# One load queue, single PSUM banks and head groups: a change to a selective-attention and MLP-mixer kernel

## The chip, the cores and the metric

The kernel runs on one core of a Trainium2 chip. The core has five engines that run side by side and wait for one another through semaphores: TensorE (PE in the profile; PEld are its weight loads), VectorE (DVE), ScalarE (ACT), GpSimd (POOL) and SyncE (SP). Transfers between memory and SBUF run on 16 DMA engines; here they are issued from two places, SP (the hardware queue, q1 in the profile) and GpSimd (the software queue, q0). Products of TensorE go to PSUM, eight banks of 512 f32 a partition, and are taken out of it by VectorE or ScalarE. The metric is device microseconds of one execution, lower is better. All times are in microseconds (us) unless another unit stands with them.

## What is computed

Eight batches, eight heads, sequence 576, head dimension 64, model dimension 512. The output of the attention is the input of a mixer block.

```
s_pos  = maximum(s, 0);  cum = cumsum(s_pos, axis=-1)
scores = q @ k^T / 8                                  # causal
scores = scores + minimum(-(cum_i - cum_j), 0)
attn   = softmax(scores)                              # 1e-9 in the denominator
x      = (attn @ v) with heads side by side           # (8, 576, 512)

h   = relu(x^T @ w_tok1) @ w_tok2                     # token mixing, 576 -> 256 -> 576
u   = x + h^T
out = u + relu(u @ w_ch1) @ w_ch2                     # channel mixing, 512 -> 1536 -> 512
```

Inputs and output are f32.

## The kernel before

**How the order is made.** The kernel does not write its instructions in order. It gives operations to a planner (`Plan`, L53): each with the engines that could do it, a cost and a latency for each, what it reads and writes, a priority, and for loads the time on the DMA engines. `Plan.run` (L103) simulates the engines and one DMA stream and picks operation after operation. The instructions are then issued in that order (L1023 to L1031), and each engine executes its own in that fixed order; semaphores keep it right when reality differs from the plan. Buffers come from rings (`Ring`, L21) of a few tiles each: `qkn` 5, `vf` 2, `E` 4, `x` 3 in SBUF, and in PSUM `psc`, two tiles of two banks (L434), and `pmx`, four tiles of one bank (L435). Where TensorE would be idle in the first 45 us of the plan, filler products of zeros are put in (L1002 to L1022).

**Work of a batch.** A quad is four heads. For each quad, one DMA from GpSimd brings k and one q, cast to bf16 (`load_cast`, L448; 288 KB written, 256 rows). TensorE transposes them in 64x64 blocks into one `psc` tile for two pairs of heads (L645); ScalarE or VectorE evicts each half (L655, L657). Scores of a pair of heads go to `psc` in two pieces (L679); ScalarE takes the exponential into `E` (L687) and VectorE applies the causal mask (L693, L701). The factor exp(cum_j) is multiplied into v instead of the scores: v comes in five chunks of 128 (the last 64) sequence rows (`vf`, L581; 256 KB and 1024 rows of 256 bytes, the last 128 KB) and is multiplied by the factor `wT` into `vp` (L590), with the factor itself as a further column (L601, L603), so that the value product (L722) gives the denominator too. The value products of two heads go into one `psc` tile, and a reciprocal (L728) and a multiplication normalise them into `x`: for batch 0 one head on VectorE (L742) and one, in five pieces, on ScalarE (L737), for later batches both in one instruction (L748).

`tok` (L792) does the token mixing: products of `w1` with x (L810), for batches 0 and 1 in two groups of four heads, relu into `h` (L820, L821), the products with `w2` in both layouts (L833 and L843 transposed, evicted at L855 and L857; L867 with the addition L874). `chan` (L906) does the channel mixing: products with `wc1` (L921), relu (L928, L930), products with `wc2` (L939), addition (L950) and store from SP (L955, L958). The channel work of a batch is what TensorE interleaves with the attention of the next.

**Queues around the change.** GpSimd issues, in this order: k and q of batch 0, then the gate, then the token weights in four pieces (512, 64, 256 and 256 rows; the keys w1, w1e, w2, w2e), wc1 in four pieces (256 rows each) and wc2 in four (384 rows each), then k and q of batches 1 to 7, and last those of batches 0 and 1 once more, for a sum of squares (L607) that a range check needs. The gate (L759) is a copy of one element of v's third chunk on GpSimd; the token weights come behind it. v is loaded by SP in all batches. For batches 1 to 7 a one-element memset of the `vf` buffer on GpSimd (L571) stands in the GpSimd order ahead of v, and the SP load waits for it. SP also issues the stores and, from batch 2 on, the transposing DMAs (L883). The load of s (L497) is the first on SP. From it come the running sum `cum`, its exponential `wn` (L516, ScalarE), and `wT` by transposes on TensorE (L524, L527). A further scan of `wn` (`pre`, L547) and four small comparisons (`gaps`, L551) belong to the same range check, which is evaluated at the end.

## Time and profile before

| what | value |
|---|---|
| time, median of 3 runs | 316.18 us (315.94 to 317.01) |
| the profiled execution's own time | 316.02 us |
| its span, first to last instruction | 314.2 us |
| granted TensorE clock, mean | 0.995 |
| DMA | 38.69 MB in 72284 packets, of which 53936 under 512 bytes |

The profile is of one execution. Busy time is the union of an engine's instructions; a row of the timeline gives start, length, engine, line, operation, tiles, shape and count, and in brackets how long the engine had been idle and what released it. A row by stage gives, for each engine, busy time and the count of instructions, then the granted clock, the DMA engines' busy share (packets that overlap count each, so it can pass 1) and GB/s written. For a DMA the page has the issuing instruction's length and, apart from it, the time from issue to landing. The share of a queue is the time that its packets took over 16 engines and the span.

### The profile page before, as it was taken

What the parts mean: (1) busy time and instruction counts of PE and PEld (TensorE: products, weight loads), DVE (VectorE), ACT (ScalarE), POOL (GpSimd) and SP (SyncE); (2) the same over time, 40 slices, a digit from 0 to 9 for tenths busy, and PEclk for the clock granted to TensorE, in tenths of its full rate; (3) what the DMA queues carried; (4) which work ended last, traced back from release to release, by engine and by line L of the source; (5) the groups of instructions that cost most, each with busy time, mean ns of one, the idle gap of its engine ahead of it and who ended that gap; (6) DMA issues with size and microseconds to landing.
All of it is one profiled execution on the core that took longest, in us unless ns stands there. A gap on an engine that the chain in (4) does not pass through costs nothing.

```text
span 314.2 us, 8013 instructions
## 1 busy us (share of the span) xinstructions
PE 293.0 (93%) x3350; PEld 168.1 (53%) x3390; DVE 168.2 (54%) x354; ACT 187.1 (60%) x315; POOL 79.5 (25%) x121
## 2 busy tenths in 40 slices
PE   4888999989999999999999999999999999999991
PEld 1446774468574455445674455446764554447540
DVE  5583235679866655586566547676425744330020
ACT  2777687858976559644783649658763356108400
POOL 5294342495247010601035010820000000000000
PEclk9999999999999999999999999999999999999997
DMA  7999999999999839346908743693003310150032
GB/s 141 180 132 204 196 198 198 214 201 248 209 203 143 180 90 216 47 100 156 187 5 132 149 104 53 102 177 121 2 0 69 102 67 2 49 136 35 1 103 73
DMA packets 72284, 38.69 MB, mean 123 GB/s; under 512 B 53936, under 2 KB 67568, under 8 KB 72240
## 3 DMA queue, kind: packets, MB, share of 16 engines
q1 hardware_dynamic: 57520, 22.57, 32.7%
q0 software_dynamic: 14720, 15.54, 31.8%
q8 instruction: 28, 0.46, 0.6%
q14 instruction: 16, 0.13, 0.1%
HBM read 40.65 MB, written 9.44 MB: 159 GB/s over the span
## 4 chain that ended last, share of the span: by engine, by line
PE 83%; DVE 6%; ACT 4%; DMA 2%; issue 2%; POOL 0%; ACTq 0%; DVEq 0%; POOLq 0%
PE pmx L939 28%; PE pmx L921 28%; PE psc L679 6%; PE pmx L810 6%; PE pmx L867 5%; PE psc L722 4%; PE psc L645 3%; DMA qkn<-in_q_dram 2%; ACT qT L655 2%; DVE qT L657 1%; ACT E L687 1%; DVE x L748 1%; DVE kT L657 1%; PE pmx L843 1%; PE pmx L1018 1%
## 5 line engine op out<-in xcount | busy, mean ns | idle before, releaser
L687 ACT ACTIVATE E<-psc 128x1024 bf16<-128x1024 f32 x64 | 62.9, 1024 | 32.6 <-PE psc L679 27.8
L921 PEld LDWEIGHTS <-wc 128*128 128x128 bf16 x624 | 58.4, 98 | 31.2 <-issue 1.0
L921 PE MATMUL pmx<-uTb,wc 128*128 128x320 bf16 (+2 forms) x384 | 55.9, 299 | 0.0
L939 PE MATMUL pmx<-wc,gb 128*128 128x512 bf16 x231 | 54.0, 379 | 0.6 <-issue 0.2
L928 ACT ACTIVATE gb<-pmx 128x320 bf16<-128x320 f32 (+2 forms) x69 | 30.3, 441 | 26.9 <-PE pmx L921 22.2
L590 POOL TENSOR_TENSOR vp<-vf,wT 128x512 bf16<-128x512 f32 (+1 forms) x35 | 36.0, 1047 | 40.0 <-issue 20.2
L921 PE MATMUL pmx<-uTa,wc 128*128 128x512 bf16 (+1 forms) x232 | 43.9, 335 | 0.8 <-issue 0.6
L939 PE MATMUL pmx<-wc,ga 128*128 128x512 bf16 x179 | 43.3, 380 | 1.2 <-issue 0.8
L607 ACT ACTIVATE junk<-qkn 128x1152 bf16<-128x1152 bf16 x32 | 37.2, 1163 | 0.4
L939 PEld LDWEIGHTS <-gb 128*128 128x128 bf16 x240 | 22.5, 98 | 25.9 <-issue 0.2
L928 ACT ACTIVATE ga<-pmx 128x512 bf16<-128x512 f32 (+1 forms) x49 | 24.2, 500 | 19.8 <-PE pmx L921 18.9
L693 DVE TENSOR_TENSOR E<-E,keep 128x512 bf16<-128x512 bf16 x64 | 28.5, 450 | 12.1 <-ACT E L687 11.9
L450 POOL DMA_DIRECT2D qkn<-in_q_dram x20 | 14.4, 718 | 59.7 <-PE psc L645 51.8
L939 PEld LDWEIGHTS <-ga 128*128 128x128 bf16 x192 | 17.3, 98 | 20.4 <-issue 1.3
L679 PE MATMUL psc<-qT,kT 64*128 64x256 bf16 (+2 forms) x320 | 23.4, 256 | 2.9 <-ACT qT L655 1.1
L722 PEld LDWEIGHTS <-E 128*128 128x128 bf16 x576 | 21.2, 97 | 8.5 <-issue 3.1
L722 PE MATMUL psc<-vp,E 128*128 128x65 bf16 x576 | 22.4, 193 | 2.8 <-ACT x L737 1.2
L748 DVE TENSOR_TENSOR x<-psc,rc 128x640 bf16<-128x640 f32 x28 | 23.1, 824 | 0.9
L679 PEld LDWEIGHTS <-kT 64*128 64x128 bf16 x320 | 12.9, 95 | 19.1 <-issue 16.5
L950 DVE TENSOR_TENSOR of<-pmx,ua 128x512 f32<-128x512 f32 x16 | 10.9, 689 | 19.1 <-PE pmx L939 19.1
L450 POOL DMA_DIRECT2D qkn<-in_k_dram x20 | 14.9, 745 | 18.4 <-issue 9.2
L810 PE MATMUL pmx<-x,w 128*128 128x512 bf16 (+1 forms) x97 | 19.2, 336 | 0.3 <-DVE x L748 0.2
(83 smaller groups left out, 263.2 us busy)
## 6 DMA issues: line engine op xcount, KB each, us to landing
vf<-in_v_dram SPq DMA_DIRECT2D x32, 256.0 KB, 6.6
out_dram<-of SPq DMA_DIRECT2D x32, 256.0 KB, 2.2
qkn<-in_k_dram POOLq DMA_DIRECT2D x20, 288.0 KB, 6.0
qkn<-in_q_dram POOLq DMA_DIRECT2D x20, 288.0 KB, 7.5
wc<-in_moe_w_ch_dram POOLq DMA_DIRECT2D x8, 384.0 KB, 11.2
vf<-in_v_dram SPq DMA_DIRECT2D x8, 128.0 KB, 5.2
out_dram<-of SPq DMA_DIRECT2D x8, 128.0 KB, 3.2
w<-in_moe_w_tok_dram POOLq DMA_DIRECT2D x2, 256.0 KB, 4.5
```

What stands on the lines that cost most here:

```text
L450: nc.gpsimd.dma_start(out=n.t[:, i, :, :], in_=src[b, h : h + 4, :, :].rearrange("(f e) (p r) d -> (e p) f (r d)", e=2, r=R))
L590: eng.tensor_tensor(out=vp.t[p0 : p0 + n, c, :, 0:D], in0=vf.t[p0 : p0 + n, c, :, :], in1=wT[p0 : p0 + n, cw, b * H : b * H + H].unsqueeze ...
L607: nc.scalar.activation(out=junk[:, :].rearrange("p (t n) -> p t n", t=2), in_=i, func=AF.Square, accum_out=sq[:, col : col + 1])
L679: nc.tensor.matmul(out=ps.t[:, hh * 512 + c0 : hh * 512 + c0 + e - a], lhsT=kT.t[hh * 64 : hh * 64 + 64, j0 : j0 + 128], rhs=qT.t[hh * 64 ...
L687: nc.scalar.activation(out=E.t[:, :, 512 * pc : 512 * pc + 512], in_=ps.t[:, :].rearrange("p (e n) -> p e n", e=2), func=AF.Exp, scale=0.125)
L693: nc.vector.tensor_tensor(out=o, in0=o, in1=keep[:, :].unsqueeze(1).unsqueeze(1).to_broadcast([128, 2, 2, 128]), op=ALU.mult)
L722: nc.tensor.matmul(out=o[:, hh, ic, 0 : D + 1], lhsT=E.t[:, hh, d0 : d0 + 128], rhs=vp.t[:, jc, h + 2 * hh, 0 : D + 1], start=(jc == j_lo) ...
L748: nc.vector.tensor_tensor(out=x.t[:, :, :].rearrange("p c (g f e d) -> p g e f c d", f=2, e=2, d=D)[:, h // 4, h % 2], in0=pav()[:, :, :, ...
L810: nc.tensor.matmul(out=pm.t[:, ha * D : hb * D], lhsT=w1[:, NJ if odd and c == NJ - 1 else c, t * 128 : t * 128 + 128], rhs=x.t[:, c, ha * ...
L921: nc.tensor.matmul(out=pm.t[:, 0 : e - a], lhsT=wc1[:, m, cc * 128 : cc * 128 + 128], rhs=uT.t[:, m, a:e], start=(m == 0), stop=(m == NMC ...
L928: lambda cc=cc, pm=pm, a=a, e=e: nc.scalar.activation(out=g.t[:, cc, a:e], in_=pm.t[:, 0 : e - a], func=AF.Relu),
L939: nc.tensor.matmul(out=pm.t[:, :], lhsT=g.t[:, cc, c * 128 : c * 128 + 128], rhs=wc2[:, cc, :], start=(cc == 0), stop=(cc == NCC - 1))
```

## The change

1. **One queue.** All loads but two go through one order on GpSimd: k and q of batch 0, v of batch 0, token weights, wc1, k and q of batch 1's first quad, half of wc2, the second quad, the other half, v of batch 1, and then per batch k/q, v, k/q. The two that stay on SP are s and the last, half-sized v chunk of batch 0, which is now SP's second load. The gate and the memsets go. In the plan each load also depends on the landing of the load eight places ahead.
2. **Single banks.** In batch 0 the transposes of one k or q go into two `pmx` tiles, one for each pair of heads, instead of one `psc` tile; the value products of the first quad go into a `pmx` tile for each head. In all of batch 0 each head has its own reciprocal and its own normalisation, on either engine (the plan's cost for ScalarE is 1.05 instead of 0.6).
3. **Token products by head groups.** In batches 0 and 1 the groups of L810 are heads 0 to 3, heads 4 and 6, heads 5 and 7; relu is done for each half of the columns, and a transposed `w2` product waits for its half alone.
4. **Smaller ones.** v products of batch 0 may go to GpSimd; `wn` has a higher priority; the copy `w1s` (L767) a later one, and even batches no longer wait for it; the scan `pre` and `gaps` are placed after the last eviction of batch 1's token stage; the planner's start time of GpSimd is 1.25 instead of 0.5.

```
-    def load_op(fn, key, us):
-        last[0] = P.op({"SP": (0.6, 0, fn)}, writes=key, prio=1, dma=us, after=last[0])
-    def cast_op(fn, key, us, occ=0.75, prio=-1):
-        last[1] = P.op({"POOL": (occ, 0, fn)}, writes=key, prio=prio, dma=us, after=last[1])
+    def load_op(fn, key, us, occ=0.75, prio=-1):
+        o = P.op({"POOL": (occ, 0, fn)}, writes=key, prio=prio, dma=us, after=chain[-1] if chain else None)
+        if len(chain) >= 8:
+            o.deps.add(chain[-8])
+        chain.append(o)
...
-        if b:
-            last[1] = P.op({"POOL": (0.1, 0.2, lambda: nc.gpsimd.memset(vf.t[0:1, 0, 0, 0:1], 0.0))},
-                           writes=[(vf, 0)], prio=-1, after=last[1])
...
             def load(c=c, n=n, p0=p0):
-                nc.sync.dma_start(out=vf.t[p0 : p0 + n, c, :, :],
+                nc.gpsimd.dma_start(out=vf.t[p0 : p0 + n, c, :, :],
                                   in_=v[b, :, c * 128 : c * 128 + n, :].rearrange("h p d -> p h d"))
+            if b == 0 and c == NJ - 1:
+                P.op({"SP": (0.6, 4.6, load_first)}, writes=[(vf, c)], prio=-2)
+                continue
...
-            pt = Buf(r_sc, False)
+            pts = [Buf(r_mx, False) for e in range(2)] if b == 0 else [Buf(r_sc, False)] * 2
...
-        pa, rc = Buf(r_sc, False), Buf(r_rc, False)
+        apart = b == 0 and h < 4
+        pas, rc = [Buf(r_mx, False) for hh in range(2)] if apart else [Buf(r_sc, False)] * 2, Buf(r_rc, False)
...
+        if b == 0:
+            for hh in range(2):
+                def rcp(hh=hh):
+                    nc.vector.reciprocal(out=rc.t[:, hh, :], in_=pav(hh)[:, :, D])
+                P.op({"DVE": (0.2, 0.25, rcp)}, reads=[(pas[hh], hh)], writes=[(rc, hh)], prio=0)
...
+                P.op({**dve(320, nrm), "ACT": (1.05, 1.2, nrm_a)}, reads=[(pas[hh], hh), (rc, hh)],
+                     writes=[(x, h + 2 * hh)], prio=-1)
+            return
...
-        heads = [(0, 4), (4, H)] if b < 2 else [(0, H)]
+        heads = [(0, 4), (4, 6), (5, 7)] if b < 2 else [(0, H)]
...
+        rgroups = [(0, 4), (4, 8)] if b < 2 else [(0, H)]
...
-    gate((vbuf[0][0], 2), lambda: vbuf[0][0].t[0:1, 2, 0, 0:1])
     load_tok()
     for i in range(4):
         load_ch1(i)
-    for i in range(4):
+    stage_qk(1, 0)
+    for i in range(2):
         load_ch2(i)
-    for b in range(1, B):
-        for h in range(0, H, 4):
-            if b > 1 or h >= AHEAD:
-                stage_qk(b, h)
-            if h == 0:
-                stage_v(b)
+    stage_qk(1, 4)
+    for i in range(2, 4):
+        load_ch2(i)
+    stage_v(1)
+    for b in range(2, B):
+        stage_qk(b, 0)
+        stage_v(b)
+        stage_qk(b, 4)
```

## What was predicted, before the result

> **What bounds the kernel now.** I read the first part of the page, then busy time by stage, then the chain of waits, and only then single rows of the first 32 us.
>
> ```profile
> PE 293.0 (93%) x3350; PEld 168.1 (53%) x3390; DVE 168.2 (54%) x354; ACT 187.1 (60%) x315; POOL 79.5 (25%) x121
> ...
> core 0: us, PE busy (x) PEld busy (x) DVE busy (x) ACT busy (x) POOL busy (x), PEclk, DMA share, GB/s
> 0.00:31.64 31.64, 23.37 (x340) 13.83 (x345) 18.37 (x58) 19.54 (x40) 17.66 (x36) 1.00 0.98 164
> 31.64:82.70 51.06, 47.65 (x719) 32.27 (x724) 31.05 (x63) 38.95 (x67) 23.41 (x34) 1.00 1.18 209
> 82.70:281.80 199.10, 196.08 (x2143) 106.93 (x2169) 114.64 (x228) 118.10 (x186) 38.43 (x52) 1.00 0.54 106
> ...
> 0.00:31.64 31.64, 9.29 (x26) 2.39 (x30) 1.00 0.98 164
> ```
>
> The last row is of the filler products of L1018 alone. TensorE is nearly full from 31.64 on: 51.06 - 47.65 = 3.4 us idle up to 82.70, 3.0 in the next 199. Before 31.64 it is busy for 23.37 us, of which 9.29 are fillers; so 14.1 us of useful work take 31.6. The kernel is bound by TensorE after 31.64, where the channel stage of batch 0 begins, and by a chain through all engines before it. What makes that point earlier is worth its whole length, as long as nothing later runs dry. The chain, and rows under it:
>
> ```profile
> 2.12 7.29 DMA qkn<-in_q_dram
> ...
> 15.64 0.77 DVE kT L657
> 16.43 0.64 ACT kT L655
> ...
> 18.16 3.72 ACT E L687 x4
> ```
>
> ```profile
> 11.92 3.82 ACT L687 ACTIVATE E<-psc 128x1024 bf16<-128x1024 f32 x4 [0.41 <-PE psc L679]
> 18.09 3.77 ACT L687 ACTIVATE E<-psc 128x1024 bf16<-128x1024 f32 x4
> 20.57 0.67 DVE L590 TENSOR_TENSOR vp<-vf,wT 64x512 bf16<-64x512 f32 x1
> 21.90 0.43 DVE L693 TENSOR_TENSOR E<-E,keep 128x512 bf16<-128x512 bf16 x1 [0.32 <-ACT E L687]
> 24.40 0.70 PE L722 MATMUL psc<-vp,E 128*128 128x65 bf16 x18 [1.16 <-ACT x L737]
> 26.05 2.17 ACT L737 ACTIVATE x<-psc,rc 128x64 bf16<-128x64 f32 x10 [0.68 <-DVE x L742]
> 31.64 0.60 PE L921 MATMUL pmx<-uTa,wc 128*128 128x256 bf16 x4
> ```
>
> The first q is waited for until 9.41, then ScalarE's exponentials set the pace, then the value products, which wait for normalisations to empty the two psc buffers, then the token stage.
>
> **The change part by part.** *What a v chunk (1024 rows of 256 bytes) costs the DMA engines.*
>
> ```profile
> q1 hardware_dynamic: 57520, 22.57, 32.7%
> q0 software_dynamic: 14720, 15.54, 31.8%
> ...
> L755 POOL DMA_DIRECT2D w<-in_moe_w_tok_dram x2: 735/738/741, 16.7 to 17.4; - x2
> w<-in_moe_w_tok_dram POOLq DMA_DIRECT2D x1, 256.0 KB, 5.4
> w<-in_moe_w_tok_dram POOLq DMA_DIRECT2D x1, 32.0 KB, 4.9
> ```
>
> On the hardware queue a packet takes 0.327 x 314.2 x 16 / 57520 = 28.6 ns, so 1024 of them 1.83 us on 16 engines; as the DMA share of 1.18 shows that packets overlap, some 1.5 us of throughput. By the same working a k or q (256 packets of the software queue's 0.318 x 314.2 x 16 / 14720 = 109 ns) is 1.5 us. The trace has no 256-byte rows on the software queue. Below stands the 32 KB piece of w2 (256 rows): it lands at 17.4 + 4.9 = 22.3, 0.2 us behind the piece before it (16.7 + 5.4 = 22.1), so 1024 rows could take 0.9. Above stands the software queue's mean packet, 5.9 us a chunk with the overlap; but those packets are mostly k's and q's long rows. I take 1.6, near the hardware queue, whose rows have the right size. The Trainium skill (DMA: Bandwidth & Descriptors, "Issuing engines are not separate DMA queues") says that transfers of all queues run on the same 16 engines and that the issuer only saves issue time; by that the chunk stays at 1.5 and the sum is the same within 0.4 us, while by the mean packet the kernel would lose time. No run here shows which holds.
>
> *What the order gives at the start.*
>
> ```profile
> 5.09 0.72 POOL L450 DMA_DIRECT2D qkn<-in_q_dram  x1
> 15.39 2.74 POOL L755 DMA_DIRECT2D w<-in_moe_w_tok_dram  x4
> 18.11 5.92 POOL L755 DMA_DIRECT2D wc<-in_moe_w_ch_dram  x8
> ...
> wc<-in_moe_w_ch_dram POOLq DMA_DIRECT2D x1, 384.0 KB, 8.1
> wc<-in_moe_w_ch_dram POOLq DMA_DIRECT2D x1, 384.0 KB, 17.2
> ...
> 15.20:17.20 2.00, 1.71 (x76) 1.05 (x78) 1.73 (x9) 1.31 (x3) 1.99 (x4) 1.00 0.14 14
> 17.30:22.30 5.00, 4.09 (x57) 2.43 (x58) 4.04 (x11) 4.57 (x6) 5.00 (x8) 1.00 1.22 157
> ```
>
> q(0,0) now lands at 2.12 + 7.29 = 9.41 beside two v chunks that SP had begun. These leave (-3.0) and the 64-row chunk, first on SP now, comes (+0.75): 7.2, so the first exponential starts at 11.92 - 2.2 = 9.7. The eight take 3.82 + 3.77 = 7.6; with one or two evictions of the second quad (0.64 each, the rest on VectorE) they end at 18.0 to 18.6, where they ended at 21.86. The second quad's k and q follow at 10.2, v's four chunks at 10.2 + 4 x 1.6 = 16.6, and the last v product (0.67) ends near 17.4 instead of 21.24.
>
> The weights: in 15.20:17.20 the DMA share is 0.14, because the gate holds w1's issue to 15.39. Without it these 2 us close. The second wc1 piece (issued at 18.82, 0.71 behind the first), which the channel stage needs first, lands 8.1 later at 26.9; less the gap, plus four chunks at 0.1 more: 25.3.
>
> *GpSimd's issue time.*
>
> ```profile
> L755 POOL DMA_DIRECT2D w<-in_moe_w_tok_dram x4: 544/738/766, 15.4 to 17.4; - x4
> POOL qkn L450 <- DMA wc<-in_moe_w_ch_dram: 8.0, 6, 2.0
> ```
>
> The four w pieces have 512, 64, 256 and 256 rows and take 0.77 down to 0.54: 0.22 for 448 rows more, so 1024 rows take about 1.1. Bounds: 0.77 if more rows cost nothing, 4 x 0.72 = 2.9 if k's and q's 256 rows scale. At 1.1 the four are out at 5.81 + 4.4 = 10.2, when the DMA needs the first at 10. Then w1 is the ninth load; the six waits of L450 on wc pieces show a load waiting for the one eight places ahead, which for w1 is the first k, long landed. Over the kernel 39 v issues add 43 us to GpSimd's 79.5 of 314: spare. Behind a waiting issue stand the next loads and, on GpSimd itself, the v products of L590; who waits for these is L722 of the next batch.
>
> *Order of the later loads:* k/q(1) go among the wc2 pieces, v(1) ahead of k/q(2).
>
> ```profile
> 50.14 3.33 SPq L581 DMA_DIRECT2D vf<-in_v_dram  x1
> vf<-in_v_dram SPq DMA_DIRECT2D x1, 256.0 KB, 10.9
> 62.34 0.23 PE L722 MATMUL psc<-vp,E 128*128 128x65 bf16 x2
> ```
>
> v(1)'s last big chunk lands at 61.0 and batch 1's first value product follows at 62.34. In the new order it needs, after 25.3, six wc pieces (13.5: the eighth, issued at 23.24, lands at 40.4), four k/q (6.0) and 4.5 chunks (7.2): 52. TensorE has batch 0's channel work until 62.3 less the gain, so 57: a margin of 4.
>
> *PSUM banks.* The transposes and four value products leave psc; counts of products and evictions stay. The wait of 1.16 ahead of 24.40 goes, and scores no longer wait for a transposed tile's eviction. The price is a reciprocal for each head:
>
> ```profile
> 25.21 0.22 DVE L728 RECIPROCAL rc<-psc 128x10 f32<-128x10 f32 x1 [1.13 <-PE psc L722]
> 25.46 0.49 DVE L742 TENSOR_TENSOR x<-psc,rc 128x320 bf16<-128x320 f32 x1
> 11.55 1.34 DVE L547 TENSOR_TENSOR_SCAN pre<-one_sb,wn 64x576 f32<-64x576 f32 x1
> ```
>
> Four more of 0.22 on VectorE, which loses the scan of 1.34 at 11.55 (moved behind batch 1's token stage; VectorE is busy there for 31.05 of 51.06, which covers it; without cover 1.3, once). A head's normalisation is 0.22 + 0.49 = 0.71 on VectorE or 2.17 / 2 = 1.08 on ScalarE. From 17.5, with two masks of 0.43 on VectorE and ScalarE free at 18.3, eight heads end at F: F - 17.5 = 0.9 + 8 x 0.71 - 0.49 x (F - 18.3) / 1.08, so 22.3. Before, x was complete at 26.05 + 2.17 = 28.2, and 3.4 later the channel stage began at 31.64. The last token group is half as wide and h is split, but TensorE's order is fixed by a plan, so I keep 3.6: 25.9. The weights' 25.3 lie just ahead of it. As the two lie so close I take 26.6: **5.0 us** earlier.
>
> *Token groups.* Ten products of 256 columns become twenty of 128, in two batches.
>
> ```profile
> 26.95 0.32 PEld L833 LDWEIGHTS <-x 128*128 128x128 bf16 x4
> 27.44 1.64 PE L810 MATMUL pmx<-x,w 128*128 128x256 bf16 x10
> ```
>
> A 128-column product is set by its weight load, 0.32 / 4 = 0.08; ten of 256 take at most 1.64, waits included. Twenty are 1.6: from nothing to 0.6 more a batch; I take 0.35, **0.7** for both. It lies on TensorE and is paid. **Idle in 31.64 to 82.70:** of 3.4 us, earlier k/q(1) and v(1) may cover some: **0.5**, of bounds 0 to 1.8.
>
> The sum against the profiled execution, 316.02 (span 314.2 and 1.8 around it): 316.0 - 5.0 + 0.7 - 0.5 = **311.2**. The median of the runs, 316.18, is 0.16 above; that is inside the rounding.
>
> **The rivals.** *Issue time scales with rows.* At 2.9 the four v issues end at 17.4, w1 goes out 2.0 later than now, wc1's second piece lands at 28.9 and the channel stage starts at 29: 316.0 - 2.6 + 0.7 - 0.5 = 313.6. For it: k/q's 0.72 at 256 rows. Against: 0.77 at 512.
>
> *VectorE holds GpSimd's issue off.* If each v issue also waits for one VectorE copy of 0.77, at the upper bound, it is 3.7: w1 out at 20.6, wc1's second piece at 32, the gain gone: 316.0 + 0.4 + 0.7 - 0.5 = 316.6. Against: in 17.30:22.30 VectorE is busy 4.04 of 5.00 and the eight wc issues beside it took 5.92 / 8 = 0.74. The Trainium skill (SBUF — State Buffer, "Who interferes with whom") states such a lock and advises the hardware queues; these rows don't show it at work.
>
> *Slower: v's rows are dear on the software queue.* The place is the v chunks ahead of the weights, and again v(1). At a price p wc1's second piece lands at 18.9 + 4p, v(1) at that + 19.5 + 4.5p, and batch 0's channel work ends 30.7 after its start. At p = 3: wc1 at 30.9, start at 31.0 (gain 0.6), v(1) at 63.9 and its products' use at 64.9, when the work has ended at 61.7: 3.2 idle. 316.0 - 0.6 + 0.7 + 3.2 = 319.3. It decides from p = 2.6, where the idle eats the gain. For it: the 109 ns mean. Against: the 32 KB piece.
>
> **How the numbers follow.** Forecast 0.56 (own range 309 to 313.5: gain 3 to 6.5, idle 0 to 1.8); issue time 0.16; held off 0.10; dear rows 0.18. A difference under 0.3%, 0.95 us, can't be told from no change. Faster holds the forecast and nearly all of the issue case: 0.71; same is most of the third: 0.09; slower 0.20. The range 308 to 317.5 leaves out most of the dear rows and the forecast's ends: together two in ten.
>
> **What would show it.** Right: the chain's wait for the first q ends near 7.2; no 1.16 ahead of a value product; a DMA share near 1 through 15 to 17; L921 from 26 to 27; v issues on GpSimd near 1.1 us; fewer idle us before L921 and no more after. Wrong: v issues over 2 us, v chunks landing more than 2.6 apart, L722 of batch 1 waiting for L590 on GpSimd, or an early start whose gain is gone again by batch 1's token stage.

## The result, and the profile after

The changed kernel takes 315.53 us (median of 18 runs, 314.95 to 316.54), the kernel before 316.13 in the same session: a ratio of 0.9974, 95% interval 0.9962 to 0.9986. So it is faster, by 0.6 us where 4.9 were forecast: clear of zero, but less than the 0.95 us below which the prediction counts a difference as no change. Here and below, medians and ratios leave out the one execution that fell into a slower state of the chip (317.23 us, run 8). The profiled execution took 315.45 us with a span of 313.7. First the page of the changed kernel: busy time, the packets, the two load queues, and the group of v's issues.

```profile
PE 294.6 (94%) x3377; PEld 169.7 (54%) x3414; DVE 171.3 (55%) x364; ACT 185.5 (59%) x309; POOL 114.7 (37%) x152
...
DMA packets 38203, 38.69 MB, mean 123 GB/s; under 512 B 17584, under 2 KB 31216, under 8 KB 38160
...
q0 software_dynamic: 17616, 24.84, 44.1%
q1 hardware_dynamic: 20544, 13.26, 17.2%
...
L572 POOL DMA_DIRECT2D vf<-in_v_dram x39 | 33.7, 872 | 6.0 <-DVE E L699 2.2
```

The bytes are the same, the packets about half. GpSimd has 35.2 us more to do, nearly all of it the 33.7 of v's issues. Now the busy time by stage, cut where the channel stage starts (28.86) and at 62; the last row is of the fillers alone.

```profile
0.00:28.86 28.86, 23.94 (x355) 14.70 (x358) 18.67 (x60) 17.71 (x34) 23.12 (x40) 0.88 1.04 184
28.86:62.00 33.14, 32.21 (x455) 20.75 (x457) 20.58 (x39) 20.18 (x37) 25.43 (x29) 1.00 1.14 227
62.00:82.70 20.70, 17.96 (x289) 12.68 (x289) 17.71 (x38) 16.16 (x27) 18.25 (x23) 1.00 0.96 195
82.70:281.80 199.10, 195.11 (x2137) 106.87 (x2162) 110.63 (x224) 120.91 (x189) 47.85 (x61) 1.00 0.51 101
...
0.00:28.86 28.86, 10.40 (x31) 2.97 (x33) 0.27 (x1) 0.88 1.04 184
```

The start is 31.64 - 28.86 = 2.8 us shorter, yet the kernel gains 0.6: 2.2 us are lost again behind it. A part of them is idle time of TensorE: 20.70 - 17.96 = 2.7 us in 62.00 to 82.70, and 4.0 in the 199.1 us after that. The same rows of the kernel before, of which the last stands with the prediction (3.0 idle):

```profile
31.64:62.10 30.46, 28.87 (x405) 17.77 (x409) 13.70 (x26) 22.96 (x42) 10.33 (x17) 1.00 1.19 201
62.10:82.70 20.60, 18.78 (x314) 14.50 (x315) 17.35 (x38) 15.99 (x26) 13.09 (x18) 1.00 1.15 221
```

Before, 62.10 to 82.70 had 1.8 idle, so 0.9 came in there and 1.0 after it. Ahead of 62 there is less, 33.14 - 32.21 = 0.9 instead of 1.6. So idle time makes up 1.2 of the 2.2 us. The rest is work: 23.94 - 10.40 = 13.5 us of useful work stand ahead of the channel stage, where it was 14.1, and the token products cost a little more (below).

The totals after 82.70 are too high in both traces. The changed kernel's has 3377 matmul records for 3414 weight loads, that of the kernel before 3350 for 3390, and a missing record can look like idle time; runs 1, 2, 5 and 10 below, with the same order of work there and all 3414 records, have 1.9 to 2.0. The difference of 1.0 stands all the same: the waits there that name another engine as releaser add up to 0.7 us before and 1.7 now.

**The start.** The chain of waits of the changed kernel, in order of time (start, length, what):

```profile
3.63 0.73 POOL identf masks.py:199
...
4.58 1.12 POOL keep masks.py:66
5.70 5.38 DMA qkn<-in_k_dram
...
16.80 3.78 ACT E L685 x4
```

The chain no longer runs through the first q, as the forecast had it, but through GpSimd's two selects (a helper that builds the identity and the triangle mask `keep`) to the second quad's k. Timelines show why: the changed kernel's GpSimd and, below it, its VectorE at that time, then the same two GpSimd instructions and the load before (start, length):

```profile
3.63 0.74 POOL masks.py:199 TENSOR_SCALAR_AFFINE_SELECT identf<-identf 64x64 f32<-64x64 f32 x1
4.58 1.17 POOL masks.py:66 TENSOR_SCALAR_AFFINE_SELECT keep<-keep 128x128 bf16<-128x128 bf16 x1
...
3.88 0.39 DVE L506 TENSOR_SCALAR s_sb<-s_sb 64x576 f32<-64x576 f32 x1
4.31 1.35 DVE L508 TENSOR_TENSOR_SCAN cum<-one_sb,s_sb 64x576 f32<-64x576 f32 x1
```

```profile
3.58 0.23 POOL masks.py:199 TENSOR_SCALAR_AFFINE_SELECT identf<-identf 64x64 f32<-64x64 f32 x1
4.03 0.40 POOL masks.py:66 TENSOR_SCALAR_AFFINE_SELECT keep<-keep 128x128 bf16<-128x128 bf16 x1
4.38 0.71 POOL L450 DMA_DIRECT2D qkn<-in_k_dram  x1
```

The first select begins 0.05 us later, takes 0.74 instead of 0.23 and ends at 4.37, behind VectorE's first step on s (3.88 to 4.27). So the second begins at 4.58 instead of 4.03 and falls beside VectorE's scan of s, which runs from 4.31 for 1.35: `keep` ends at 5.75, 0.09 behind the scan. The load behind it goes out at 5.70 instead of 4.38. The Trainium skill (SBUF — State Buffer, "Who interferes with whom") states an exclusive lock between a VectorE instruction with two SBUF inputs and a GpSimd instruction that reads SBUF, in which whoever is second waits for the whole of the first. The rows of the second select agree: 0.40 alone, 1.17 beside the scan. Whether the two meet hangs on hundredths of a microsecond: in the traces of runs 9, 15 and 16 below, which leave these instructions as they are, the selects took 0.23 and 0.39 to 0.40, and the load went out at 4.37 to 4.41.

**The stage at 62 to 83.** VectorE's masks, GpSimd and TensorE in the timeline of the changed kernel:

```profile
70.67 1.06 DVE L691 TENSOR_TENSOR E<-E,keep 128x512 bf16<-128x512 bf16 x1
...
72.32 1.06 DVE L699 TENSOR_TENSOR E<-E,keep 128x128 bf16<-128x128 bf16 x1
...
73.64 0.41 DVE L691 TENSOR_TENSOR E<-E,keep 128x512 bf16<-128x512 bf16 x1
...
70.19 1.06 POOL L584 TENSOR_TENSOR vp<-vf,wT 128x512 bf16<-128x512 f32 x1
71.18 0.93 POOL L572 DMA_DIRECT2D vf<-in_v_dram  x1
72.12 1.17 POOL L584 TENSOR_TENSOR vp<-vf,wT 128x512 bf16<-128x512 f32 x1
...
75.78 0.39 PE L677 MATMUL psc<-qT,kT 64*128 64x256 bf16 x4 [1.48 <-ACT qT L653]
```

A mask that takes 0.41 alone takes 1.06 where a v product (L584) of GpSimd began first; the small one of 0.22 takes 1.06 too. ScalarE's eviction of qT, on which the scores at 75.78 wait, stood behind VectorE's eviction of the same tile, and that behind the masks. TensorE idles 1.48 us. Masks (tiles E and keep) and products (vf, wT and vp) have no tile in common, so neither waits for the other's result; it is the mask itself that takes longer. (The expectations below speak of shared buffers; no row shows one.) How full GpSimd is shows in one stretch, before and after (GpSimd is the last of the five pairs):

```profile
42.00:80.00 38.00, 34.65 (x617) 22.53 (x620) 25.49 (x52) 29.39 (x45) 20.41 (x28) 1.00 1.16 213
```

```profile
42.00:80.00 38.00, 35.46 (x495) 23.55 (x498) 28.18 (x50) 22.48 (x37) 36.95 (x43) 1.00 1.03 219
```

From 20.41 to 36.95 of 38.00: for these 38 us GpSimd is hardly ever idle, though over the whole span it is busy for 37%.

### The profile page after: what moved, and what is told of

Its sections match the earlier page's. It is cut to its first block, busy times and chain, and to the rows that moved or that the text cites. A ratio compares the mean times of both kernels' runs of the same rounds, so it can differ in the third digit from the quotient of the medians.

```text
span 313.7 us, 8025 instructions
## 1 busy us (share of the span) xinstructions
PE 294.6 (94%) x3377; PEld 169.7 (54%) x3414; DVE 171.3 (55%) x364; ACT 185.5 (59%) x309; POOL 114.7 (37%) x152
## 2 busy tenths in 40 slices
DMA packets 38203, 38.69 MB, mean 123 GB/s; under 512 B 17584, under 2 KB 31216, under 8 KB 38160
## 3 DMA queue, kind: packets, MB, share of 16 engines
q0 software_dynamic: 17616, 24.84, 44.1%
## 4 chain that ended last, share of the span: by engine, by line
PE 73%; DVE 13%; ACT 5%; issue 3%; DMA 2%; POOL 1%; POOLq 0%; ACTq 0%
PE pmx L954 27%; PE pmx L936 25%; PE pmx L818 5%; PE psc L725 5%; PE psc L677 4%; PE pmx L880 3%; DVE ua L887 2%; ACT E L685 2%; PE psc L643 2%; DMA qkn<-in_k_dram 2%; DVE E L691 2%; DVE qT L655 2%; DVE kT L655 1%; DVE E L699 1%; ACT qT L653 1%
## 5 line engine op out<-in xcount | busy, mean ns | idle before, releaser
L936 PEld LDWEIGHTS <-wc 128*128 128x128 bf16 x624 | 57.7, 98 | 32.2 <-issue 1.4
L936 PE MATMUL pmx<-uTb,wc 128*128 128x320 bf16 (+2 forms) x384 | 56.7, 299 | 0.0
L584 POOL TENSOR_TENSOR vp<-vf,wT 128x512 bf16<-128x512 f32 (+1 forms) x35 | 36.9, 1064 | 27.7 <-PE psc L725 27.0
L936 PE MATMUL pmx<-uTa,wc 128*128 128x512 bf16 (+1 forms) x233 | 44.9, 336 | 0.9 <-issue 0.5
L943 ACT ACTIVATE gb<-pmx 128x320 bf16<-128x320 f32 (+2 forms) x66 | 28.9, 441 | 24.4 <-PE pmx L936 20.0
L954 PEld LDWEIGHTS <-gb 128*128 128x128 bf16 x240 | 22.3, 98 | 25.7 <-issue 0.4
L572 POOL DMA_DIRECT2D vf<-in_v_dram x39 | 33.7, 872 | 6.0 <-DVE E L699 2.2
L943 ACT ACTIVATE ga<-pmx 128x512 bf16<-128x512 f32 (+1 forms) x41 | 20.9, 516 | 14.4 <-PE pmx L936 14.1
L954 PEld LDWEIGHTS <-ga 128*128 128x128 bf16 x192 | 18.0, 98 | 20.7
L677 PEld LDWEIGHTS <-kT 64*128 64x128 bf16 x320 | 13.4, 96 | 18.9 <-issue 16.4
L725 PE MATMUL psc<-vp,E 128*128 128x65 bf16 x540 | 21.0, 193 | 0.3 <-ACT E L685 0.3
L818 PE MATMUL pmx<-x,w 128*128 128x512 bf16 (+2 forms) x116 | 19.4, 306 | 1.0 <-ACT h L830 0.4
```

What stands on the lines that cost most here:

```text
L572: nc.gpsimd.dma_start(out=vf.t[p0 : p0 + n, c, :, :], in_=v[b, :, c * 128 : c * 128 + n, :].rearrange("h p d -> p h d"))
L584: eng.tensor_tensor(out=vp.t[p0 : p0 + n, c, :, 0:D], in0=vf.t[p0 : p0 + n, c, :, :], in1=wT[p0 : p0 + n, cw, b * H : b * H + H].unsqueeze ...
L677: nc.tensor.matmul(out=ps.t[:, hh * 512 + c0 : hh * 512 + c0 + e - a], lhsT=kT.t[hh * 64 : hh * 64 + 64, j0 : j0 + 128], rhs=qT.t[hh * 64 ...
L725: nc.tensor.matmul(out=o[:, ic, 0 : D + 1], lhsT=E.t[:, hh, d0 : d0 + 128], rhs=vp.t[:, jc, h + 2 * hh, 0 : D + 1], start=(jc == j_lo), st ...
L818: nc.tensor.matmul(out=cols(pm.t[:, :], ha, hb), lhsT=w1[:, NJ if odd and c == NJ - 1 else c, t * 128 : t * 128 + 128], rhs=cols(x.t[:, c, ...
L936: nc.tensor.matmul(out=pm.t[:, 0 : e - a], lhsT=wc1[:, m, cc * 128 : cc * 128 + 128], rhs=uT.t[:, m, a:e], start=(m == 0), stop=(m == NMC ...
```

## The experiments

The theory after this reading had two parts. A: the second quad's loads, held up by the selects, shorten the gain of the start. B: what the start gains is eaten in 62 to 83 us, because GpSimd's products hold VectorE's masks off. Rivals were that ScalarE or the fixed order sets that stage's pace, that the moved scan does, that the token groups cost it, and that the end follows the start one for one. All kernels are edits of the changed one. The kernel before took 316.07, 315.88, 316.01 and 316.15 us in the four sessions. Ratios are to it, in the same session; they are estimated from the single runs and can differ a little from the quotient of the medians. The last column is from one profiled execution of each kernel. Runs 2, 5, 6 and 10 have the first batch of the changed kernel without an edit, and there the channel stage starts at 27.93 to 30.55: a difference of less than some 2.6 us in that column doesn't show the effect of an edit by itself.

| kernel | median us | ratio, 95% interval | channel stage starts |
|---|---|---|---|
| changed kernel | 315.53 | 0.9974 (0.9962 to 0.9986) | 28.86 |
| 1 mask late | 315.27 | 0.9966 (0.9952 to 0.9981) | 27.50 |
| 2 scan late | 315.53 | 0.9977 (0.9962 to 0.9991) | 30.55 |
| 3 both | 314.80 | 0.9948 (0.9927 to 0.9969) | 27.65 |
| 4 token groups undone | 316.30 | 0.9996 (0.9974 to 1.0018) | 28.36 |
| 5 products narrow | 312.60 | 0.9891 (0.9863 to 0.9919) | 27.93 |
| 6 squares narrow | 315.22 | 0.9979 (0.9965 to 0.9994) | 28.90 |
| 7 loads later | 317.03 | 1.0027 (1.0012 to 1.0043) | 30.78 |
| 8 3 and 5 together | 312.52 | 0.9874 (0.9838 to 0.9911) | 29.01 |
| 9 v from SP | 321.05 | 1.0146 (1.0123 to 1.0169) | 29.27 |
| 10 masks out | 313.41 | 0.9921 (0.9900 to 0.9942) | 28.55 |
| 11 products apart | 314.17 | 0.9942 (0.9921 to 0.9963) | 27.41 |
| 12 planned anew | 311.64 | 0.9866 (0.9846 to 0.9886) | 26.59 |
| 13 as 12, mask early | 311.80 | 0.9847 (0.9813 to 0.9880) | 26.76 |
| 14 as 12, 0.75 us | 314.41 | 0.9939 (0.9913 to 0.9965) | 27.65 |
| 15 0.88 us alone | 312.68 | 0.9883 (0.9845 to 0.9920) | 26.30 |
| 16 banks undone | 319.17 | 1.0066 (1.0037 to 1.0094) | 33.66 |

**1 to 3: the start and the scan.** In 1 the triangle mask is built behind v's first issue, in v's `load`:

```
     def identities():
...
-        make_upper_triangular(nc, keep, val=1.0, diag=True)
...
+                if b == 0 and c == 0:
+                    make_upper_triangular(nc, keep, val=1.0, diag=True)
```

In 2 the scan `pre` and `gaps` run just ahead of the last comparison, and their places in the plan stay as empty operations:

```
+    P.op({"DVE": (1.3, 1.6, lambda: None)},
+        reads=["wn", "late"], writes=["pre"], prio=50)
+    P.op({"DVE": (0.5, 0.8, lambda: None)}, reads=["pre", "wn", "cum"], writes=["bad0"], prio=50)
+    def check_all():
+        nc.vector.tensor_tensor_scan(
+            out=pre[:, :], data0=one_sb[:, :], data1=wn[:, 0:S], initial=0.0, op0=ALU.mult, op1=ALU.add)
+        gaps()
...
+    P.op(dve(64, check_all),
```

3 has both. The order of all else stays.

> The changed kernel with the causal mask 'keep' made on GpSimd behind the issue of v's first chunk instead of ahead of the second quad's k and q; TensorE's order is the same. Theory A (VectorE's scan of s and GpSimd's selects exclude each other, and this holds back the second quad's loads): the selects ahead of the loads no longer reach into the scan, the second k is issued near 4.5 instead of 5.70 and lands 1 to 1.3 earlier, the channel stage of batch 0 starts 0.8 to 1.3 earlier than 28.86. Rival B (the 1.17 us select has another cause): the mask's select still takes 0.7 or more, at its new place, and the loads gain less than 0.5. For the end: if a lead of the start carries through, the ratio to the kernel before is 0.994 (another -1.1 us); if VectorE and ScalarE set the pace of 62 to 83 us, it stays at 0.997.

> The changed kernel with the moved scan 'pre' and its four comparisons run just ahead of the last check (near 225 us or later) instead of at 78 us; TensorE's order is the same. If the scan on a full VectorE costs time (it took 2.02 us at 78.07, and TensorE then stood still for 0.77 at 81.14): that wait goes and the time falls by 0.5 to 2 us, ratio 0.991 to 0.996. If it was covered, as the prediction had it: no change, 0.997.

> e1 and e2 together. If both effects are real and carry through, they add: -1.1 and about -0.8, ratio 0.991. If the stage of 62 to 83 us swallows the start's lead, only e2's part is left.

Run 1 did what part A says: the loads go out at 4.31 and 5.02 instead of 5.70 and 6.41, and the channel stage starts 1.4 us earlier in its trace. (By the means of the traces it is 0.9: 28.96 for the changed kernel and runs 2, 5, 6 and 10 with the loads late, 28.05 for runs 1, 3 and 8 with them early.) But the end moves by 0.3. Its TensorE and GpSimd near 75 us:

```profile
42.05 1.80 POOL L571 DMA_DIRECT2D vf<-in_v_dram  x2 [2.24 <-DVE ga L946]
...
75.65 1.33 POOL L585 TENSOR_TENSOR vp<-vf,wT 128x512 bf16<-128x512 f32 x1
...
75.67 0.61 PE L678 MATMUL psc<-qT,kT 64*128 64x256 bf16 x4 [1.83 <-ACT qT L654]
```

The idle piece has grown from 1.48 to 1.83 and ends at 75.67, 0.11 from where it ended in the changed kernel. GpSimd's queue stands still as well. In the changed kernel:

```profile
29.11 0.93 POOL L572 DMA_DIRECT2D vf<-in_v_dram  x1 [0.72 <-DMA qkn<-in_k_dram]
...
42.02 1.80 POOL L572 DMA_DIRECT2D vf<-in_v_dram  x2 [2.22 <-DVE E L699]
...
75.76 1.32 POOL L584 TENSOR_TENSOR vp<-vf,wT 128x512 bf16<-128x512 f32 x1
```

v's load starts at 42.02 and that product at 75.76. Between these two times GpSimd pauses once, for 0.50, so an earlier start of the channel stage doesn't move it, and the masks keep to its times. The row names a VectorE mask as the releaser, and that of run 1 another instruction; but the time is that of a landing: the first chunk of v(1), issued at 29.11, landed 12.9 us later, at 42.0. In runs 1, 2, 5, 7, 10, 12, 13 and 15 the two times agree as well, at 41.7 to 43.5, with a DMA share of 1.19 or 1.20 in 20 to 42 us. So far as the traces show, it is the loads that set it.

Moving the scan (2) changed nothing that can be measured in the time. In its trace the start is 1.7 us later than in the changed kernel's; the masks of 60 to 83 us take 453 and 212 ns, and TensorE idles there for 0.6 us instead of 2.7. A later start lost less behind it. Both edits together (3) are 0.7 us faster than the changed kernel, with overlapping intervals.

**4: token groups.** In batches 0 and 1 the last two groups are one again, planned anew.

```
-        heads = [(0, 4), (4, 6), (5, 7)] if b < 2 else [(0, H)]
+        heads = [(0, 4), (4, H)] if b < 2 else [(0, H)]
```

> The changed kernel with the token products of batches 0 and 1 in two groups of four heads again (relu still by halves; the plan is made anew, so the order differs a little elsewhere). If the finer groups cost what was predicted, 0.7 us of TensorE, and give back some in the first batch: -0.7 to +0.5, ratio 0.995 to 0.999. If the half-size last group matters at the start: the channel stage starts 0.5 to 1 later and the time is up by as much.

It is 0.8 us slower by the medians, with overlapping intervals, and TensorE idles for 2.91 us at 72. With a new plan the groups' own price isn't told apart from the order's.

**5, 6, 8 and 10: who is late in 62 to 83.** In 5 GpSimd's products are cut, in 6 ScalarE's squares, in 10 the masks (`mk` and `mk4`), in this order below; 8 is 5 with both edits of 3.

```
+                m = D if b < 2 else 8
-                    out=vp.t[p0 : p0 + n, c, :, 0:D], in0=vf.t[p0 : p0 + n, c, :, :],
+                    out=vp.t[p0 : p0 + n, c, :, 0:m], in0=vf.t[p0 : p0 + n, c, :, 0:m],
```

```
-        nc.scalar.activation(out=junk[:, :].rearrange("p (t n) -> p t n", t=2), in_=i, func=AF.Square,
+        nc.scalar.activation(out=junk[:, :].rearrange("p (t n) -> p t n", t=2)[:, :, 0:16], in_=i[:, :, 0:16],
+                             func=AF.Square, accum_out=sq[:, col : col + 1])
```

```
+                if b > 1:
+                    return
```

> Changed kernel, same order of work; from the third batch on GpSimd's value scaling covers 8 of each head's 64 columns (the other 56 are left unscaled from an earlier batch, so the output of batches 2 to 7 is not the reference's). GpSimd then holds the buffers it shares with VectorE for far less of 62 to 83 us. Theory (GpSimd's products hold VectorE's masks off there, and that turns the earlier start back into idle time): the long masks return to 0.41 and 0.22 us, TensorE's idle pieces of 1.48 and 0.77 us go, the time falls by 1 to 2.5 us to 313.0 to 314.5. Rival (another engine, ScalarE or the fixed order itself, sets the pace of that stage): the masks shorten, the time stays within 0.5 us of 315.5.

> Changed kernel, same order of work; ScalarE's range check squares 16 of 64 columns (the rest of the check is left out; the output stays the reference's). Each drops from 1.17 us to about 0.4. Theory of the shared buffers: ScalarE was not last, the 1.48 us idle piece stays because the qT eviction waits for a late VectorE, time 315 to 315.7. Rival (ScalarE's 16 us of 20.7 set the pace of 62 to 83 us): 313.5 to 314.7.

> Mask made behind v's first load, scan of the counts moved to the end, and the narrow products of the third batch on together. The start is 1.2 us earlier than in the changed kernel. Theory: with the products short the lead of the start reaches the end, 314.8 minus 1 to 2.5: 312.3 to 313.8. Rival: 314.3 to 315.3, no more than without the narrow products.

> Changed kernel, same order of work, GpSimd's products whole again; from the third batch on VectorE's triangle masks are left out (the output of batches 2 to 7 is not the reference's). Theory (it is VectorE, waiting for buffers that GpSimd's product holds, that is late in 62 to 83 us): without the masks VectorE has nothing that waits there except the scan, the idle pieces of 1.48 and 0.77 us go, 312.3 to 313.6, as with the narrow products (312.6). Rival (GpSimd's own pace, its products and loads being late, set the end): 314.7 to 315.6.

Run 5 gained 2.9 us, more than the theory asked. The groups of VectorE in 60 to 83 us, kernel before, changed kernel and then run 5 (count, busy us, mean ns, idle before):

```profile
L693 DVE TENSOR_TENSOR E<-E,keep 128x512 bf16<-128x512 bf16 x5 | 2.3, 460 | 0.0
L701 DVE TENSOR_TENSOR E<-E,keep 128x128 bf16<-128x128 bf16 x2 | 0.4, 218 | 0.0
```

```profile
L691 DVE TENSOR_TENSOR E<-E,keep 128x512 bf16<-128x512 bf16 x6 | 3.1, 516 | 0.0
L699 DVE TENSOR_TENSOR E<-E,keep 128x128 bf16<-128x128 bf16 x3 | 2.3, 778 | 0.0
L1002 DVE TENSOR_TENSOR_SCAN pre<-one_sb,wn 64x576 f32<-64x576 f32 x1 | 2.0, 2024 | 0.0
```

```profile
L692 DVE TENSOR_TENSOR E<-E,keep 128x512 bf16<-128x512 bf16 x6 | 2.5, 410 | 0.3 <-ACT E L686 0.3
L1003 DVE TENSOR_TENSOR_SCAN pre<-one_sb,wn 64x576 f32<-64x576 f32 x1 | 1.3, 1340 | 0.0
L700 DVE TENSOR_TENSOR E<-E,keep 128x128 bf16<-128x128 bf16 x3 | 0.7, 248 | 0.0
```

Run 5 has the same instructions as the changed kernel and 2.9 us less of VectorE, and both idle pieces are gone. But narrow products also relieve GpSimd itself. Run 10 tells these apart: there GpSimd is as full as before (first row, 36.98 of 38.00) and only VectorE's masks are gone, and still TensorE's idle time in 62.00 to 82.70 falls from 2.7 to 0.4 us (second row):

```profile
42.00:80.00 38.00, 37.51 (x515) 24.43 (x513) 26.64 (x53) 24.71 (x40) 36.98 (x43) 1.00 1.04 218
...
62.00:82.70 20.70, 20.32 (x321) 14.08 (x320) 16.59 (x34) 17.38 (x30) 18.07 (x22) 1.00 0.97 196
```

So it is the meeting of masks and products, not GpSimd's lateness for TensorE. Run 10 alone could also be VectorE's relief from the masks' own time, but in run 5 VectorE keeps all of its instructions. What both leave as it is are the 1.9 to 2.0 us of idle time in 82.70 to 281.80, with or without masks there: the 1.0 us that came in behind 82.70 has another cause, and it stays open. In run 6 the squares are a fraction and the idle pieces of 1.78 and 0.82 us are still there, at 315.22: ScalarE doesn't set that stage's pace. Run 8 came out as the theory had it, in three executions (311.69 to 313.91).

**7: a later start.** The mask is built three times ahead of the loads.

```
+        for _ in range(3):
+            make_upper_triangular(nc, keep, val=1.0, diag=True)
```

> Changed kernel, the upper-triangle mask made three times instead of once before the second quad's loads, everything else the same: those loads go out some 1 to 2 us later and the channel stage of the first batch starts about that much later (30 to 31 instead of 28.9). Theory (the start's lead is eaten before 150 us whatever its size): the end moves by under a third of the delay, 315.5 to 316.2. Rival (the start sets the end one for one): 316.8 to 317.5.

A miss: the channel stage started 1.9 us later and the end came 1.5 later. The lead is lost, a delay is not: in this run GpSimd's product of 75.76 also came 1.5 us later, at 77.30. What stands at 76 us is the later of two chains: v's load went out at 43.50 here, again with the landing of v(1)'s first chunk.

**9: v from SP.**

```
-                nc.gpsimd.dma_start(out=vf.t[p0 : p0 + n, c, :, :],
+                (nc.gpsimd if b == 0 else nc.sync).dma_start(out=vf.t[p0 : p0 + n, c, :, :],
```

> Changed kernel, same order of work, but v of batches 1 to 7 is issued by SyncE again (v of batch 0 stays on GpSimd). GpSimd is rid of 34 issues of 0.87 us, 5 of them in 62 to 83 us; v's rows go back to single 256-byte packets. Theory (GpSimd's products hold VectorE's masks off, and the issues of v between them spread the products over the stage): GpSimd's products come earlier and closer, masks are held off less, 313.5 to 315.0. Rival (the products collide with the masks wherever they are, or v's dearer packets give the gain back): 315.2 to 316.5.

A miss on both sides, 5.5 us slower. Nothing holds SP's queue back now: the first four chunks of v(1) go out from 2.12 on, the first two ahead of the second quad's k and q, and TensorE then waits for batch 1's k (SP's queue, then TensorE):

```profile
2.12 9.18 SPq L572 DMA_DIRECT2D vf<-in_v_dram  x4
...
35.07 0.48 PE L643 MATMUL psc<-ident,qkn 64*64 64x64 bf16 x36 [2.58 <-DMA qkn<-in_k_dram]
```

So this run doesn't test the issues' time alone. It shows what the common order holds in place.

**11 and 12: kernels that keep all of the work.** Both have the mask late and the scan planned as part of the final check, and the planner is told 0.88 us for an issue of v, as the trace has it, where the change had 0.75. Run 11 also makes the products of batch b+1 wait for the last mask of batch b; the last two lines are its alone.

```
-            load_op(load, [(vf, c)], 1024 * 0.0226 / 16 * n / 128)
+            load_op(load, [(vf, c)], 1024 * 0.0226 / 16 * n / 128, occ=0.88)
...
+                for o in vops.get(b + 1, ()):
+                    o.deps.add(mo)
```

> A kernel that computes everything: the mask made behind v's first load, the scan of the counts at the end, the planner told 0.88 us for an issue of v, and the value products of batch b+1 held back until batch b's last mask, so that GpSimd's products and VectorE's masks of one stage do not meet; the order of work is planned anew. Theory: no mask takes over 0.6 us in 60 to 83 us, the start's lead lasts, 312.8 to 314.3. Rival (the held-back products are late for the value products of the next batch, and TensorE waits for them): 315.5 to 318.

> As the kernel with the products held back, without the holding back: mask late, scan at the end, 0.88 us for an issue of v, planned anew. It tells what the new plan alone does. Theory: some masks still meet products, 314.0 to 315.3. Rival (the plan alone matters): the same time as with the products held back, within 0.3 us.

Run 11 took the masks to 0.46 and 0.22 us and the idle piece away, but later products came late: TensorE waits 1.07 us at 193.72 and 0.38 at 117.73 for a mask ahead of value products. Run 12 beat it, outside both expectations: 311.64, 4.4 us faster than the kernel before.

**13 to 15: which alteration did it.** 13 is run 12 with the mask early, 14 is run 12 with 0.75, 15 is the changed kernel with 0.88 and no other edit.

> The newly planned kernel (311.6 us) with the upper-triangle mask back ahead of the second quad's loads, as in the changed kernel; plan and order are those of the newly planned kernel. The channel stage should start 1.2 to 1.5 us later than its 26.6. Theory (once nothing eats the lead, the start counts one for one): 312.6 to 313.3. Rival (the start's lead is still eaten): within 0.4 us of 311.6.

> The newly planned kernel with the planner told 0.75 us for an issue of v, as in the changed kernel, instead of the 0.88 that the trace shows; mask late and scan at the end stay. Theory (the plan placed products against masks as if GpSimd were faster than it is, so they met): long masks and an idle piece of over 1 us come back in 60 to 83 us, 313.5 to 315. Rival (the scan's removal from the plan made the gain): 311.3 to 312.3.

> The changed kernel with one number of its planner altered: 0.88 us instead of 0.75 for an issue of v; mask ahead of the second quad's loads and scan in the middle as before. Theory (issue time in the plan decides whether masks and products meet): 312.3 to 313.8. Rival: 314.8 to 316.

One number of the planner makes nearly 3 us: 15 gains 2.9 with it alone, 14 loses 2.3 (by the ratios) to 2.8 against run 12 without it, and the rest of run 12 adds 0.5 to 1. In 14 the idle piece of 1.83 is back at 75.81; in 15 one of 1.23 at 71.47 is the largest left, and TensorE idles for 1.9 us in 62.00 to 82.70 instead of 2.7. Two groups of run 15 in 60 to 83 us:

```profile
L691 DVE TENSOR_TENSOR E<-E,keep 128x512 bf16<-128x512 bf16 x6 | 4.5, 766 | 0.0
L699 DVE TENSOR_TENSOR E<-E,keep 128x128 bf16<-128x128 bf16 x3 | 0.6, 214 | 0.0
```

So the new order doesn't keep masks and products apart: the small masks are free, the long ones wait longer than in the changed kernel. It has them wait where less hangs on it. More is gained at the start: of the 3.9 us between the two profiled spans (313.7 and 309.8), 2.6 lie ahead of the channel stage (26.30). The loads that went out at 4.37 in that trace are hardly the reason, since run 13 has them at 5.69 and starts at 26.76. Which of the many moved instructions does how much wasn't taken apart, and no third value was tried: whether 0.88 helps because it is the measured time, or because another order happens to be better, isn't shown. Run 13 missed on its premise: with the loads issued 1.4 us later the channel stage started only 0.2 later.

**16: banks undone.**

```
-            pts = [Buf(r_mx, False) for e in range(2)] if b == 0 else [Buf(r_sc, False)] * 2
+            pts = [Buf(r_sc, False)] * 2
-        apart = b == 0 and h < 4
+        apart = False
```

> The changed kernel with the first batch's transposes and value products back in double banks (the pool of two), planned anew. Theory (the banks let the first batch run ahead of its evictions): exps end 1 us or more later than 20.6, the channel stage starts 0.8 to 2 us later than 28.9, time 315.8 to 317. Rival (the banks are worth nothing at the start, the loads are last): channel stage within 0.5 us of 28.9, time 315 to 316.

3.6 us slower than the changed kernel (316.85 to 320.09, a wide scatter), more than either side expected, and slower than the kernel before; the channel stage starts 4.8 us later, although the loads went out at 4.37. Value products wait for normalisations again:

```profile
24.38 0.70 PE L725 MATMUL psc<-vp,E 128*128 128x65 bf16 x18 [0.85 <-DVE x L737]
26.44 1.15 PE L725 MATMUL psc<-vp,E 128*128 128x65 bf16 x18 [0.98 <-DVE x L737]
```

## Why the prediction was wrong

The direction and the mechanism of the start were right; the forecast missed by 4.3 us, in two steps of about equal size: 2.2 at the start (2.8 of 5.0), and 2.0 behind it (2.2 lost where the sum had 0.2). In the first the second quad's loads and the completion of x were too late for the sum's terms; in the second idle time came in where the sum took some off.

- **v's price on the software queue: right, and the bound above was far off.** 1.6 us a chunk was taken; chunks landed 1.0 to 1.6 us apart in batches 0 and 1. The mean packet, 5.9 us a chunk, was no guide: the software queue got 17616 - 14720 = 2896 more packets for 24.84 - 15.54 = 9.30 MB, 3.2 KB each. The rows were joined. With that the dear-rows rival falls.
- **Issue time: near.** 1.1 us taken, 0.87 measured; the rival that it scales with rows (2.9) falls. The 39 issues cost 33.7 us instead of 43.
- **"GpSimd's 79.5 of 314: spare" and "idle -0.5, bounds 0 to 1.8": the step that failed for the second half.** It took the average of the span for a stage. In 42 to 80 us 17.6 of 38.00 were free, and 16.5 of them were filled (v's 15 issues there take 13.0). The prediction named who is queued behind an issue (the next loads, the v products), but not that a product holds up VectorE's masks while it runs, nor that the order would bring the two together. Run 10, with GpSimd as full but the masks out, shows that the fullness alone cost nothing; with run 5 it shows the cause in 62 to 83 us, where 0.9 us of idle time came in. Over the term's own stretch, from the channel stage's start to 82.70, idle time went from 3.4 to 0.9 + 2.7 = 3.7 us (unrounded 0.93 + 2.74): +0.3 instead of -0.5. For what comes behind 82.70 the sum had no term; +1.0 came in there, and the runs don't show why.
- **VectorE against GpSimd.** The rival had the lock at the wrong place. It looked for it between evictions and weight issues, and priced it there at 316.6. It acted on the selects at 3.63 and 4.58 and, the other way round, on the masks. That the time came near that rival's is chance.
- **The first loads: half right.** q(0,0) was to land at 7.2 and the first exponential to start at 9.7; they came at 8.18 and 10.34.
- **The second quad, "10.2", and the exponentials, "18.0 to 18.6": failed.** Its k and q landed at 11.07 and 12.58, and the exponentials ended at 16.80 + 3.78 = 20.58. The prediction let the loads follow in the DMA queue and didn't ask what stood ahead of them on GpSimd. What the late loads alone are worth is not sized: 0.9 us by the means of the traces, in a scatter of 2.6. In this execution the granted clock was 0.74 in 5 to 18 us, but that isn't shown to be the cause either, since runs 5, 10 and 2, with the same first batch at a clock of 1.00, start at 27.93, 28.55 and 30.55. Nor do early loads give the forecast's times: in runs 1, 12 and 15, with the loads at 4.31 to 4.37, the exponentials end at 18.9 to 19.2. Run 13 has the loads late and starts at 26.76, so in another order they cost nearly nothing.
- **x complete at "22.3": failed in this kernel, reached in another order.** It was 24.79 + 0.49 = 25.28, 4.7 us behind the last exponential, because the order gives ScalarE five more pieces (23.62, 1.14 long) and the last head to VectorE behind them. In run 15 it was complete at 22.45, 3.5 behind the exponentials.
- **"I keep 3.6": right.** 28.86 - 25.28 = 3.6.
- **Weights and v(1): right.** wc1's second piece landed at 23.61, ahead of the 25.3, v(1) at 46.5, ahead of 52. The DMA gap of 15.20 to 17.20 closed (share 0.14 before, 1.31 after).
- **Banks: right in the mechanism.** No value product waits 1.16 for a normalisation any more, and with the banks undone (16) waits of 0.85 and 0.98 are back and the kernel is slower than before. As 16 is planned anew, the banks' own share of its 3.6 us isn't known.
- **Scan "covered": right in its effect.** It ran for 2.02 instead of 1.34 beside a product, but run 2 shows no gain from moving it.
- **Token groups, 0.7: too high.** These products took 5.4 us in batches 0 and 1 before (40 of 256 columns); now 20 of 256 and 40 of 128 columns take 2.7 + 3.0 = 5.7 us, so the price is 0.3. Undoing the groups costs 0.8, but in another plan.

In run 12 the sum's times are reached: the channel stage at 26.59 where 26.6 was predicted, and 311.64 us where 311.2 was. The start that was forecast is thus within this kernel's reach. But it takes another order than the change has, and masks and products still meet there: the long masks of 60 to 83 us take 718 ns, and TensorE idles for 1.8 us in 62.00 to 82.70. So the agreement to 0.4 us is in part luck. That one number did most of it was found by experiment, not foreseen.

## What to carry to other kernels

Room on an engine is counted in the stage where the new work lands, not over the span, and together with whom the engine shuts out while it works. Where a planner fixes the order, a changed instruction's cost is worth setting to what the trace shows before the change is judged: 0.88 in place of 0.75 us moved this kernel's time by 2.9, nearly five times the change's own gain. A new plan can move it by as much for other reasons, so one value doesn't prove the rule. An earlier start is worth its length only up to the next chain that doesn't begin at the start.

## What the runs showed of the hardware that was not expected

- Rows of 256 bytes went in packets of 3.2 KB on average on GpSimd's software queue, where SP's hardware queue moved them in packets of their own: 38203 packets instead of 72284. The Trainium skill (DMA: Bandwidth & Descriptors, "Issuing engines are not separate DMA queues") says that issuing from several engines only saves the time of initiating the transfers. That all share the same 16 engines isn't contradicted here, but the issuer did change the packets.
- A shift of 0.05 us of GpSimd's selects against VectorE's instructions on s went with 1.3 us: 4.38 or 5.70 for the load behind them.
- A VectorE mask can be held for longer than one product. In run 1 one that began during an issue of v lasted from 69.42 to 71.64, to the end of the product behind that issue (70.09 to 71.14) and on; alone it takes 0.41. An issue by itself doesn't hold it: in the changed kernel the mask at 73.64 ran beside issues (73.25 to 75.74) in 0.41. Why it is held so long was not settled.
- In the profiled execution of the changed kernel the granted clock fell to about half in the second fortieth of the span, in those of runs 6 and 8 too; in that of the kernel before it did not. Busy time in 5 to 18 us with the granted clock (third number from the end), and 36 transposes, in the changed kernel and in run 5:

```profile
5.00:18.00 13.00, 10.58 (x199) 5.83 (x201) 8.66 (x18) 8.21 (x11) 11.87 (x18) 0.74 1.17 208
...
13.18 0.70 PE L643 MATMUL pmx<-ident,qkn 64*64 64x64 bf16 x36
```

```profile
5.00:18.00 13.00, 10.54 (x207) 5.85 (x209) 9.07 (x19) 9.03 (x12) 11.81 (x19) 1.00 1.17 211
...
12.69 0.48 PE L644 MATMUL pmx<-ident,qkn 64*64 64x64 bf16 x36 [0.63 <-DMA qkn<-in_q_dram]
```

The same 36 transposes take 0.70 and 0.48 us. What brings the lower clock on was not settled.
